# The last 64 rows of two batches in one block, rows dealt in twos, three ways of adding x, and late rows of y moved by DMA

## The chip, the cores and the metric

The kernel runs on one core of a Trainium2 chip. The metric is the device time of one execution in microseconds, the median of several runs. Times of kernels that ran at different sittings are compared through the kernel before, which ran in each: by their ratios to it, where 0.001 is 0.45 us.

## The reference, cut to what matters

```
# attention with forget gates: 8 batches, 8 heads, 576 rows, head size 64
scores = scale * q k^T + (cum_i - cum_j), causal;  attn = softmax(scores);  x = attn v
# then, with x as [8 batches, 576 rows, 512]:
X = rfft(x, axis=1)[:, :64];  Y = X * (w_r + i w_i) per mode      # 64 modes, 512 x 512 each
y = irfft(Y, n=576)
u = x + y
out = u + max(u @ w_ch, 0)
```

576 is four and a half blocks of 128 partitions. That half block, per batch, is what the change is about. The weights of the modes are read from memory at 512 KB per load, 128 loads or so.

## The kernel before: the parts that matter

Attention runs in 32 steps (one head of two batches each). In each step the products of the exponentials E and v make x, block by block:

```
def emit_av(s, sbs):                       # sbs = [0, 1, 2], then [3, 4]
    for i, sb in enumerate(sbs):
        for h in range(2):                 # the two batches
            for jb in range(sb + 1):
                c = EOFF[jb] + (sb - jb) * 128
                nc.tensor.matmul(pav[:, i, h, :], lhsT=E[:, h, c : c + 128],
                                 rhs=va[:, jb, h, :], ...)
    # x_all[:, batch, sb, ...] = pav * 1 / (sum of the row)
```

That is 1+2+3+4+5 = 15 products for each batch. While attention runs, GpSimd issues the loads of q, k, v and of the weights, in order. The weights go into a ring of nine buffers. A buffer comes free when the modes that use it have been multiplied, and the first modes wait for the first spectrum, at step 9 of attention:

```
for s in range(NS + 1):
    if h == 0 and pr + STG - 1 < NPR:  emit_loads(pr + STG - 1)       # q, k, v
    if s < 10 and nload < min(NRING, 3 + 3 * s // 4):  next_w()       # fills the ring
    if s == 10:  pool_dma(wch[:], ...)                                # w_ch, 512 KB
    # ... transposes, scores, emit_av, DFT of this step ...
    if s > B:
        while nmode < (s - B) * NTH // (NS - B):
            emit_modes(nmode); nmode += 1
            next_w()                                                  # needs a free buffer
```

The output stage comes last, when the last modes are done. Modes 0 to 15 come late ("late rows" of y: 32 rows for each batch), are transposed and multiplied for four batches at once into the PSUM tile `pl`, and are copied from there, batch by batch, by VectorE and ScalarE between the output jobs. A job makes two blocks, or the half block, of `out`:

```
def emit_rows(b, pl):
    nc.vector.tensor_copy(yy[0:32, b, 0, :], pl[0][rows, :])
    nc.scalar.copy(yy[0:32, b, 1, :], pl[1][rows, :])

def emit_out(b, sb0, nb, by_pool, ps):
    # pu += basis^T yy[b, 0];  pz += basis^T yy[b, 1]   (u = x + y;  z = u @ w_ch)
    if by_pool:                                    # type P below
        nc.vector.tensor_tensor(u_sb, pu, x_all[...], ALU.add)
        nc.scalar.activation(o_sb, pz, ACT.Relu)
        nc.gpsimd.tensor_tensor(o_sb, o_sb, u_sb, ALU.add)
    else:                                          # type N: x was added by an identity product
        nc.scalar.copy(u_sb, pu)
        nc.vector.scalar_tensor_tensor(o_sb, pz, 0.0, u_sb, ALU.max, ALU.add)
    nc.sync.dma_start(out[b, 128*sb0 : 128*sb0+256, :].rearrange("(r p) e -> p r e", r=2), o_sb)

jobs = [(b, sb0, nb) for b in range(B) for sb0, nb in ((0, 2), (2, 2), (4, 1))]   # 24 jobs
for n, job in enumerate(jobs):
    emit_out(*job, ...)
    if n == 8: pl = emit_late(1); emit_rows(4, pl)
    if n in (0, 1, 2, 9, 10, 11): emit_rows(n + 1 if n < 3 else n - 4, pl)
```

Each job fills two PSUM tiles of two banks; there are four such tiles in all, and `pl` takes one of them.

The softmax here doesn't subtract the row's maximum and nothing guards it: scores larger than these inputs give would overflow.

## Time and profile before

| | |
|---|---|
| time | 452.51 us (451.94 to 452.87, 4 runs) |
| span of the profiled run | 449.9 us |
| last weights used by TensorE | 403.24 us |
| last vector operation ends | 441.59 + 1.81 = 443.40 us |

I divide the span at these two points: the **load stream** up to the last weights, the **output stage** (40.2 us here), and the **drain**, in which stores land and the engines meet (6.5 us).

The chain of waits on the page of the profile, which follows back what released what, is mostly DMA:

```profile
DMA 81%; PE 10%; DVE 2%; issue 2%; ACT 2%; POOL 0%; DVEq 0%; POOLq 0%; ACTq 0%
```

In the views PE is TensorE, PEld its loads of weights, DVE VectorE, ACT ScalarE, POOL GpSimd and SP SyncE. The windows view gives, for stretches of the span, each engine's busy time and instruction count, the granted TensorE clock (PEclk, 1.00 is full speed), the DMA share and the rate. First the load stream:

```profile
core 0: us, PE busy (x) PEld busy (x) DVE busy (x) ACT busy (x) POOL busy (x), PEclk, DMA share, GB/s
0.00:76.00 76.00, 50.90 (x633) 34.45 (x633) 61.78 (x169) 54.37 (x79) 28.67 (x46) 1.00 1.16 226
76.00:104.00 28.00, 23.28 (x444) 18.11 (x444) 21.61 (x59) 18.70 (x29) 12.52 (x17) 0.94 1.18 207
104.00:396.00 292.00, 204.55 (x3404) 148.81 (x3413) 127.56 (x347) 114.16 (x176) 88.24 (x123) 0.76 1.17 217
```

The late rows, the output stage and the drain:

```profile
403.20:408.30 5.10, 4.60 (x27) 2.21 (x28) 1.19 (x3) 0.58 (x2) 0.00 (x0) 0.50 0.01 3
408.30:443.40 35.10, 30.87 (x136) 13.18 (x137) 26.51 (x30) 24.82 (x31) 25.16 (x14) 1.00 0.65 230
443.40:449.90 6.50, 0.00 (x0) 0.00 (x0) 0.00 (x1) 0.00 (x0) 0.00 (x0) 0.69 0.66 216
```

No engine is full in the output stage; TensorE is nearest to it. What it waited for, by the waits view after 403 us (total, times, longest), was mostly ScalarE:

```profile
PE pz L739 <- ACT uo L764: 1.7, 3, 0.7
PE A L134 <- DMA wb<-in_moe_w_i_dram: 1.1, 1, 1.1
PE pl L710 <- DVE YTl L149: 0.5, 1, 0.5
PE pz L739 <- ACT uo L767: 0.4, 1, 0.4
PE pz L739 <- DVE uo L768: 0.2, 1, 0.2
```

The timeline of GpSimd near 64 to 79 us (start, duration, what; in brackets the idle time before it and what ended it) shows the last load for the ninth weights buffer going out at 64.44, and then no load for 13.8 us, until TensorE has used the first buffer:

```profile
64.44 0.74 POOL L84 DMA_DIRECT2D wb<-in_moe_w_i_dram  x1 [1.75 <-DMA wb<-in_moe_w_r_dram]
78.97 0.74 POOL L84 DMA_DIRECT2D wb<-in_moe_w_r_dram  x1 [13.79 <-PE tp L426]
```

### The profile page before, as it was taken

The page shows a single profiled execution, that of the slowest core. Times are in us where ns is not written, and L with a number is a line of the kernel's source. Part 1 is how long each engine was busy: PE and PEld are TensorE (multiplying, and loading weights), DVE is VectorE, ACT ScalarE, POOL GpSimd, SP SyncE. Part 2 cuts the span into 40 slices and gives each one's busy share as a digit, 9 for nine tenths or more (in the row PEclk, how much of TensorE's full clock was granted, in tenths as well). Part 3 has the DMA queues.
Part 4 walks back from the last instruction along what each step waited for, and adds up shares of the span by engine and source line. Part 5 has one row for each costly group of instructions (what it writes and reads, how often), then busy time and mean ns, then how long its engine had stood idle before and what let it go on. Part 6 is the DMA issues. An engine that isn't in the chain of part 4 may idle for free.

```text
span 449.9 us, 10945 instructions
## 1 busy us (share of the span) xinstructions
PE 317.4 (71%) x4688; PEld 218.9 (49%) x4704; DVE 239.0 (53%) x608; ACT 212.6 (47%) x313; POOL 154.6 (34%) x200
## 2 busy tenths in 40 slices
PE   2398877695975968859578879999722257248992
PEld 1255556474754646647556656556512234233441
DVE  5769998684864745747467853233100012105873
ACT  3388988565654654545356614443200012006672
POOL 7333330553333333332333322322232323102783
PEclk9999999987778786786687969999855569558998
DMA  8999999999999999999999999999999999963677
GB/s 204 206 234 233 233 233 233 201 214 228 213 232 221 220 233 216 224 233 206 233 233 211 211 211 211 211 211 211 211 211 211 211 211 211 211 124 106 223 267 247
DMA packets 68144, 96.80 MB, mean 215 GB/s; under 512 B 3264, under 2 KB 44736, under 8 KB 68096
## 3 DMA queue, kind: packets, MB, share of 16 engines
q0 software_dynamic: 62480, 85.34, 102.4%
q1 hardware_dynamic: 5536, 10.63, 6.8%
q8 instruction: 37, 0.61, 0.5%
q10 hardware_dynamic: 80, 0.13, 0.2%
q14 instruction: 11, 0.09, 0.1%
HBM read 163.73 MB, written 9.44 MB: 385 GB/s over the span
## 4 chain that ended last, share of the span: by engine, by line
DMA 81%; PE 10%; DVE 2%; issue 2%; ACT 2%; POOL 0%; DVEq 0%; POOLq 0%; ACTq 0%
DMA wb<-in_moe_w_i_dram 42%; DMA stk<-in_k_dram 18%; DMA stq<-in_q_dram 11%; DMA wb<-in_moe_w_r_dram 7%; DMA stv<-in_v_dram 3%; PE pz L739 2%; PE pu L751 2%; PE pz L751 1%; PE A L134 1%; PE tp L426 1%; ACT uo L767 1%; PE pav L512 1%; PE ps L478 1%; PE pu L734 1%; PE pl L714 1%
## 5 line engine op out<-in xcount | busy, mean ns | idle before, releaser
L485 ACT ACTIVATE E<-ps 128x1024 bf16<-128x1024 f32 (+1 forms) x128 | 103.7, 868 | 28.4 <-PE ps L478 19.7
L134 PE MATMUL A<-XT,wb 128*128 128x16 bf16 x2048 | 71.8, 172 | 50.6 <-DMA wb<-in_moe_w_i_dram 29.5
L134 PEld LDWEIGHTS <-wb 128*128 128x128 bf16 x2048 | 64.3, 100 | 64.3 <-DMA wb<-in_moe_w_i_dram 32.5
L84 POOL DMA_DIRECT2D wb<-in_moe_w_r_dram x65 | 47.3, 728 | 131.7 <-DMA wb<-in_moe_w_r_dram 29.7
L84 POOL DMA_DIRECT2D wb<-in_moe_w_i_dram x65 | 47.2, 727 | 80.0 <-DMA wb<-in_moe_w_i_dram 45.8
L478 PE MATMUL ps<-QTs,KT 64*128 64x64 bf16 (+4 forms) x384 | 56.8, 313 | 10.3 <-ACT E L485 9.5
L149 DVE TENSOR_TENSOR YT<-A,Yacc 128x128 bf16<-128x128 f32 x24 | 8.9, 369 | 77.9 <-PE A L134 77.9
L512 PE MATMUL pav<-va,E 128*128 128x65 bf16 x960 | 48.5, 204 | 0.9 <-DVE va L456 0.4
L512 PEld LDWEIGHTS <-E 128*128 128x128 bf16 x960 | 40.6, 105 | 11.8 <-issue 8.2
L439 ACT COPY KT<-tp 128x640 bf16<-128x640 bf16 (+1 forms) x32 | 22.3, 748 | 39.1 <-PE tp L426 39.1
L500 DVE TENSOR_TENSOR E<-E,trimask 128x256 bf16<-128x256 bf16 (+2 forms) x128 | 38.4, 316 | 3.9 <-ACT E L485 3.7
L657 ACT CAST XW<-pxw 128x512 bf16<-128x512 f32 x40 | 22.7, 587 | 31.6 <-PE pxw L650 26.6
L426 PE MATMUL tp<-ident_bf,kb 128*128 128x128 bf16 x144 | 16.3, 270 | 30.0 <-DVE kb L410 29.5
L650 PE MATMUL pxw<-wch,yy 128*128 128x512 bf16 x152 | 35.4, 380 | 1.3 <-issue 1.1
L765 POOL TENSOR_TENSOR uo<-uo 64x512 f32<-64x512 f32 (+1 forms) x14 | 25.2, 1810 | 28.8 <-DVE uo L761 25.9
L669 ACT CAST yy<-pyw 128x512 bf16<-128x512 f32 x8 | 4.7, 586 | 59.1 <-PE pyw L662 57.6
L521 DVE TENSOR_TENSOR x_all<-pav,rcp 128x384 bf16<-128x384 f32 x64 | 31.4, 490 | 1.0
L478 PEld LDWEIGHTS <-KT 64*128 64x128 bf16 x384 | 18.4, 97 | 22.8 <-issue 14.0
L426 PEld LDWEIGHTS <-kb 128*128 128x128 bf16 x144 | 11.7, 121 | 33.7 <-DVE kb L410 30.8
L443 ACT COPY VT<-tp 128x640 bf16<-128x640 bf16 (+1 forms) x32 | 22.5, 754 | 11.0 <-PE tp L426 10.7
L410 DVE COPY kb<-stk 128x1152 bf16<-128x1152 bf16 x16 | 7.9, 495 | 34.2 <-DMA stk<-in_k_dram 34.1
L441 DVE COPY QTs<-tp 128x640 bf16<-128x640 bf16 (+1 forms) x32 | 23.2, 766 | 5.0 <-PE tp L426 4.1
(103 smaller groups left out, 481.0 us busy)
## 6 DMA issues: line engine op xcount, KB each, us to landing
wb<-in_moe_w_r_dram POOLq DMA_DIRECT2D x63, 512.0 KB, 17.2
wb<-in_moe_w_i_dram POOLq DMA_DIRECT2D x63, 512.0 KB, 18.0
out_dram<-uo SPq DMA_DIRECT2D x16, 512.0 KB, 3.0
stv<-in_v_dram POOLq DMA_DIRECT2D x14, 576.0 KB, 15.7
stk<-in_k_dram POOLq DMA_DIRECT2D x16, 288.0 KB, 15.7
stq<-in_q_dram POOLq DMA_DIRECT2D x16, 288.0 KB, 15.6
stv<-in_v_dram SPq DMA_DIRECT2D x2, 576.0 KB, 6.9
out_dram<-uo SPq DMA_DIRECT2D x7, 128.0 KB, 2.4
```

Of the source, the lines that this page charges most:

```text
L84: tc.keep_in_program_order(nc.gpsimd.dma_start(dst, src))
L134: nc.tensor.matmul(A[:, eb, mi, :], lhsT=wb[:, t, mi, r * D + eb * 128 : r * D + (eb + 1) * 128], rhs=XT3[:, m, c0 : c0 + 2 * B], start=(i ...
L426: nc.tensor.transpose(tp[:, r - r0, :, :].rearrange("c h p -> c (h p)"), sb[:, r, :, :].rearrange("p b d -> p (b d)"), ident_bf[:, :],)
L441: nc.vector.tensor_copy(rows(QT[pr][:, :, :]), tv)
L478: nc.tensor.matmul(ps[:, b, o : o + n], lhsT=KTs[pr % 2][bs, h, jb * 128 : (jb + 1) * 128], rhs=QT[pr][bs, h, jb * 128 + c0 : jb * 128 + c ...
L485: nc.scalar.activation(E[:, :, piece * 512 : piece * 512 + w], ps[:, :, 0:w], ACT.Exp, scale=scale,)
L500: nc.vector.tensor_tensor(dg, dg, tr, ALU.mult)
L512: nc.tensor.matmul(pav[:, i, h, :], lhsT=E[:, h, c : c + 128], rhs=va[:, jb, h, :], start=(jb == 0), stop=(jb == sb),)
L521: nc.vector.tensor_tensor(x_all[:, 2 * bp : 2 * bp + 2, sbs[0] : sbs[0] + n, dc * 128 + hd * Dh : dc * 128 + (hd + 1) * Dh,].rearrange("p ...
L650: nc.tensor.matmul(pxw[:, :], lhsT=xT[:, eb, sb * 128 : (sb + 1) * 128], rhs=wch[:, eb, :], start=(eb == 0), stop=(eb == NDC - 1),)
L657: nc.scalar.copy(XW[:, b, sb, :], pxw[:, :])
L765: nc.gpsimd.tensor_tensor(o_sb, o_sb, u_sb, ALU.add)
```

## The change

Its intent, as I read it:

- The last 64 rows of two batches share one block of 128 partitions: 20 output jobs instead of 24, and nine blocks of x and of x W for a pair of batches instead of ten.
- Rows of a pair of blocks are dealt in twos (partition p holds rows 2p and 2p+1), so that a store writes runs of 4 KB instead of 2 KB. The price is in attention: E is read with a stride of two, and a block of even or odd rows needs an extra half-width product. 17 products for each batch instead of 15.
- Jobs have types. The code knows four; three are used, 9 N (5 large, 4 shared), 7 P and 4 W. W adds x and applies the maximum on VectorE alone.
- The late rows for batches 1 to 7 go from PSUM to SBUF in one copy for four batches and then by DMA, SBUF to SBUF, to their partitions.

The diff, cut to its core:

```
 def emit_av(s, sbs):
+    for i, sb in enumerate(sbs):
+        if sb == 4:                                   # the shared block, half-width
+            for jb in range(NSB):
+                c = EOFF[jb] + (4 - jb) * 128
+                narrow += [(2, b, b, jb, c, 64, 1) for b in range(2)]
+            continue
+        k2, r = sb & 2, sb & 1
+        for b in range(2):
+            for jb in range(k2 + 1):
+                c = EOFF[jb] + (k2 - jb) * 128 + r
+                wide_.append((2 * i + b, b, 0, jb, c, 128, 2))      # stride 2
+            narrow.append((2 * i + b, b, 1, k2 + 1, EOFF[k2 + 1] + r, 64, 2))
 [...]
+def emit_late_rows(q4, pl):
+    nc.vector.tensor_copy(yl[:, 0, :], pl[0][:, :])
+    nc.scalar.copy(yl[:, 1, :], pl[1][:, :])
+    for j in range(1 - q4, 4):
+        nc.sync.dma_start(yy[0:32, 4 * q4 + j, :, :], yl[32 * j : 32 * j + 32, :, :])
 [...]
+    if sb == 4:
+        for h in range(2):
+            nc.tensor.matmul(p[64 * h : 64 * h + 64, 0, :], lhsT=BI[:, 512:576],
+                             rhs=yy[:, b + h, t, :], ...)
 [...]
+    if ty in "PW": nc.vector.tensor_tensor(u_sb, pu, xblk(x_all, job), ALU.add)
+    else:          nc.scalar.copy(u_sb, pu)
+    if ty in "PQ": # ScalarE Relu, GpSimd add, as P before
+    else:          nc.vector.scalar_tensor_tensor(o_sb, pz, 0.0, u_sb, ALU.max, ALU.add)
-    out[b, 128 * sb0 : 128 * sb0 + 256, :].rearrange("(r p) e -> p r e", r=2)
+    out[b, 128 * sb : 128 * sb + 256, :].rearrange("(p r) e -> p r e", r=2)
 [...]
+jobs = [(*j, ty) for j, ty in zip(jobs, "NPWPNPWPNNPWPNNPWNNN")]
+emit_rows(0, pl); emit_late_rows(0, pl)
+for n, job in enumerate(jobs):
+    emit_out(...)
+    if n == 3: emit_late_rows(1, emit_late(1))
```

The rest (a sixth block of the basis, iota, indices of x) follows from these.

More of the change, by code (lines that the diff above doesn't have):

```diff
@@ L48, with xi @@
     EOFF = [0, 576, 1024, 1344, 1536]
-    EW = 1664
+    EW = 1600
+    NX = 9
+    def xi(b, sb):
+        return (b % 2) * 3 + sb if sb < 3 else 6 + b % 2 if sb == 3 else 8
     RP = 64
@@ L59 @@
     xtpool = ctx.enter_context(tc.tile_pool(name="xtpool", bufs=3))
-    x_all = xpool.tile([128, B, NSB, D], BF16, name="x_all")
+    x_all = xpool.tile([128, B // 2, NX, D], BF16, name="x_all")
     Yacc = xpool.tile([128, NDC, NM, 2 * B], F32, name="Yacc")
@@ L65 @@
     wch = const.tile([128, NDC, D], BF16, name="wch")
-    bas = const.tile([128, NSB, NM, 2], BF16, name="bas")
+    bas = const.tile([128, NSB + 1, NM, 2], BF16, name="bas")
     BI = const.tile([128, SP], BF16, name="BI")
@@ L257 @@
         emit_w_load(1)
-        s_i = ssb.tile([128, NSB], I32, name="s_i")
+        s_i = ssb.tile([128, NSB + 1], I32, name="s_i")
         tc.keep_in_program_order(
-            nc.gpsimd.iota(s_i[:], pattern=[[128, NSB]], base=0, channel_multiplier=1)
+            nc.gpsimd.iota(
+                s_i[:, 0:4], pattern=[[256, 2], [1, 2]], base=0, channel_multiplier=2
+            )
+        )
+        tc.keep_in_program_order(
+            nc.gpsimd.iota(
+                s_i[:, 4:6], pattern=[[-64, 2]], base=512, channel_multiplier=1
+            )
         )
@@ L270 @@
             nc.vector.memset(t[:, :, S:SP], 0.0)
-        for t in Es:
-            nc.vector.memset(t[:, :, EW - 64 : EW], 0.0)
         lf = ft
@@ L350, in emit_basis @@
             TURN = 2.0 * math.pi / S * (1.0 - 2.0e-7)
-            s_f = ssb.tile([128, NSB], F32, name="s_f")
+            NB1 = NSB + 1
+            s_f = ssb.tile([128, NB1], F32, name="s_f")
             nc.vector.tensor_copy(s_f[:], s_i[:])
@@ L354, in emit_basis @@
             nc.vector.tensor_copy(m_f[:], m_i[:])
-            ang = wide[:, 0 : 2 * NSB * NM].rearrange(
-                "p (a b c) -> p a b c", a=2, b=NSB
+            ang = wide[:, 0 : 2 * NB1 * NM].rearrange(
+                "p (a b c) -> p a b c", a=2, b=NB1
             )
-            rnd = scratch(128, 2, NSB, NM)
+            rnd = scratch(128, 2, NB1, NM)
             nc.vector.tensor_tensor(
                 ang[:, 1, :, :],
-                _strided(s_f[:, 0:1], [[1, NSB], [0, NM]]),
-                _strided(m_f[:, 0:1], [[0, NSB], [1, NM]]),
+                _strided(s_f[:, 0:1], [[1, NB1], [0, NM]]),
+                _strided(m_f[:, 0:1], [[0, NB1], [1, NM]]),
                 ALU.mult,
@@ L378, in emit_basis @@
             Zt = rnd[:, :, :, :].rearrange("p a b c -> p (a b c)").rearrange(
-                "p (s m t) -> p s m t", s=NSB, m=NM
+                "p (s m t) -> p s m t", s=NB1, m=NM
             )
@@ L383, in emit_basis @@
             nc.vector.memset(Zt[64:128, 4, :, :], 0.0)
+            nc.vector.memset(Zt[0:64, 5, :, :], 0.0)
             nc.vector.tensor_copy(bas[:, :, :, :], Zt[:, :, :, :])
@@ L506, in emit_av @@
             n = len(sbs)
-            pav = psO.tile([128, 3, 2, Dh + 1], F32, tag="av", name="pav")
+            pav = psO.tile([128, 6, Dh + 1], F32, tag="av", name="pav")
+            wide_, narrow = [], []
             for i, sb in enumerate(sbs):
-                for h in range(2):
-                    for jb in range(sb + 1):
-                        c = EOFF[jb] + (sb - jb) * 128
-                        nc.tensor.matmul(
-                            pav[:, i, h, :],
-                            lhsT=E[:, h, c : c + 128],
-                            rhs=va[:, jb, h, :],
-                            start=(jb == 0),
-                            stop=(jb == sb),
-                        )
@@ L519, in emit_av @@
-            rcp = nrm.tile([128, 3, 2, 1], F32, tag="rcp", name="rcp")
-            nc.vector.reciprocal(rcp[:, 0:n, :, :], pav[:, 0:n, :, Dh : Dh + 1])
-            nc.vector.tensor_tensor(
-                x_all[
-                    :,
-                    2 * bp : 2 * bp + 2,
-                    sbs[0] : sbs[0] + n,
-                    dc * 128 + hd * Dh : dc * 128 + (hd + 1) * Dh,
-                ].rearrange("p b c d -> p c b d"),
-                pav[:, 0:n, :, 0:Dh],
-                _strided(rcp[:, 0, 0, 0:1], [[2, n], [1, 2], [0, Dh]]),
-                ALU.mult,
-            )
+                if sb == 4:
[3 more added lines that the diff above has]
+                    continue
@@ new lines, in emit_av @@
+                k2, r = sb & 2, sb & 1
[4 more added lines that the diff above has]
+                    narrow.append((2 * i + b, b, 1, k2 + 1, EOFF[k2 + 1] + r, 64, 2))
+            for n, (slot, b, half, jb, c, w, st) in enumerate(wide_ + narrow):
+                nc.tensor.matmul(
+                    pav[64 * half : 64 * half + w, slot, :],
+                    lhsT=E[:, b, c : c + (w - 1) * st + 1 : st],
+                    rhs=va[:, jb, b, :],
+                    start=(n == 0),
+                    stop=(n == len(wide_) + len(narrow) - 1),
+                    skip_group_check=True,
+                )
@@ new lines, in emit_av @@
+            ns = 6 if sbs[0] == 0 else 3
+            d0 = dc * 128 + hd * Dh
+            rcp = nrm.tile([128, 6, 1], F32, tag="rcp", name="rcp")
+            nc.vector.reciprocal(rcp[:, 0:ns, :], pav[:, 0:ns, Dh : Dh + 1])
+            if ns == 6:
+                xo = x_all[:, bp, 0:6, d0 : d0 + Dh].rearrange(
+                    "p (b c) d -> p c b d", b=2
+                )
+                pi = pav[:, :, 0:Dh].rearrange("p (c b) d -> p c b d", b=2)
+                ri = _strided(rcp[:, 0, 0:1], [[2, 3], [1, 2], [0, Dh]])
+            else:
+                xo = x_all[:, bp, 6:9, d0 : d0 + Dh]
+                pi = pav[:, 0:3, 0:Dh]
+                ri = _strided(rcp[:, 0, 0:1], [[1, 3], [0, Dh]])
@@ L533, in emit_dft @@
+            nc.vector.tensor_tensor(xo, pi, ri, ALU.mult)
         def emit_dft(pr):
@@ L547, in emit_dft @@
                             px[:, :, :],
-                            lhsT=_strided(x_all[:, b, sb, d0 : d0 + 1], [[st, 128]]),
-                            rhs=bas[:, sb, :, :],
+                            lhsT=_strided(
+                                x_all[:, bp, xi(b, sb), d0 : d0 + 1], [[st, 128]]
+                            ),
+                            rhs=bas[:, sb if sb < 4 else 4 + b % 2, :, :],
                             start=(sb == 0),
@@ L615 @@
         late["YT"], late["YTl"] = YT, YTl
-        XW = bsb.tile([128, B, NSB, D], BF16, name="XW")
+        XW = bsb.tile([128, B // 2, NX, D], BF16, name="XW")
         yy = bsb.tile([128, B, 2, D], BF16, name="yy")
@@ L634, with emit_xw @@
             )
-            def emit_xw(b):
-                xT = xTs[b % 3]
+            def emit_xw(n):
+                bp, i0, nb = n // 2, (0, 5)[n % 2], (5, 4)[n % 2]
+                xT = xTs[n % 3]
                 for eb in range(NDC):
                     ptr = psBig.tile([128, SP], BF16, tag="big", name="ptr")
-                    for sc in range(NSB):
+                    for i in range(nb):
                         nc.tensor.transpose(
-                            ptr[:, sc * 128 : (sc + 1) * 128],
-                            x_all[:, b, sc, eb * 128 : (eb + 1) * 128],
+                            ptr[:, i * 128 : (i + 1) * 128],
+                            x_all[:, bp, i0 + i, eb * 128 : (eb + 1) * 128],
                             ident_bf[:, :],
                         )
-                    nc.vector.tensor_copy(xT[:, eb, :], ptr[:, :])
-                for sb in range(NSB):
+                    nc.vector.tensor_copy(
+                        xT[:, eb, 0 : nb * 128], ptr[:, 0 : nb * 128]
+                    )
+                for i in range(nb):
                     pxw = psBig.tile([128, D], F32, tag="big", name="pxw")
@@ L651, in emit_xw @@
                             pxw[:, :],
-                            lhsT=xT[:, eb, sb * 128 : (sb + 1) * 128],
+                            lhsT=xT[:, eb, i * 128 : (i + 1) * 128],
                             rhs=wch[:, eb, :],
@@ L656, in emit_xw @@
                         )
-                    nc.scalar.copy(XW[:, b, sb, :], pxw[:, :])
+                    nc.scalar.copy(XW[:, bp, i0 + i, :], pxw[:, :])
             def emit_y(b):
@@ L721, in emit_late @@
             return ply, plw
+        yls = {}
         def emit_rows(b, pl):
@@ L726, in emit_rows @@
             nc.scalar.copy(yy[0:32, b, 1, :], pl[1][rows, :])
-        def emit_x(b, sb0, nb, by_pool):
+        def emit_late_rows(q4, pl):
+            yl = xtpool.tile([128, 2, D], BF16, tag="XT3", name="yl")
+            nc.vector.tensor_copy(yl[:, 0, :], pl[0][:, :])
+            nc.scalar.copy(yl[:, 1, :], pl[1][:, :])
+            for j in range(1 - q4, 4):
+                nc.sync.dma_start(
+                    yy[0:32, 4 * q4 + j, :, :], yl[32 * j : 32 * j + 32, :, :]
+                )
@@ L730, in emit_x, with xblk @@
+        def xblk(t, job):
+            b, sb, nb, _ = job
+            i0 = xi(b, sb)
+            step = xi(b, sb + 1) - i0 if nb == 2 else 1
+            return _strided(t[:, b // 2, i0, 0:1], [[step * D, nb], [1, D]])
+        def emit_x(job):
+            b, sb, nb, ty = job
             pu = psZ.tile([128, 2, D], F32, tag="z", name="pu")
             pz = psZ.tile([128, 2, D], F32, tag="z", name="pz")
-            for i in range(nb):
-                if not by_pool:
-                    nc.tensor.matmul(
-                        pu[:, i, :], lhsT=ident_bf[:, :], rhs=x_all[:, b, sb0 + i, :],
-                        start=True, stop=False,
-                    )
@@ L738, in emit_x @@
-            for i in range(nb):
-                nc.tensor.matmul(
-                    pz[:, i, :], lhsT=ident_bf[:, :], rhs=XW[:, b, sb0 + i, :],
-                    start=True, stop=False,
-                )
-            return pu, pz
-        def emit_out(b, sb0, nb, by_pool, ps):
-            Ms = 64 if nb == 1 else 128
-            pu, pz = ps
-            for t, p in enumerate((pu, pz)):
+            for p, t in ((pu, x_all), (pz, XW)):
+                if t is x_all and ty not in "NQ":
+                    continue
@@ L749, in emit_out @@
                 for i in range(nb):
-                    sb = sb0 + i
                     nc.tensor.matmul(
                         p[:, i, :],
-                        lhsT=BI[:, sb * 128 : (sb + 1) * 128],
-                        rhs=yy[:, b, t, :],
-                        start=(t == 0 and by_pool),
-                        stop=True,
-                    )
-            uo = wpool.tile([128, 2, 2, D], F32, tag="wb", name="uo")
-            u_sb, o_sb = uo[:Ms, 0, 0:nb, :], uo[:Ms, 1, 0:nb, :]
@@ L760, in emit_out @@
-            if by_pool:
-                nc.vector.tensor_tensor(
-                    u_sb, pu[:Ms, 0:nb, :], x_all[:Ms, b, sb0 : sb0 + nb, :], ALU.add
-                )
-                nc.scalar.activation(o_sb, pz[:Ms, 0:nb, :], ACT.Relu)
+                        lhsT=ident_bf[:, :],
+                        rhs=t[:, b // 2, xi(b, sb + i), :],
+                        start=True,
+                        stop=False,
+                        skip_group_check=True,
+                    )
+            return pu, pz
@@ new lines, in emit_out @@
+        def emit_out(job, ps, last):
+            b, sb, nb, ty = job
+            for t, p in enumerate(ps):
+                fresh = t == 0 and ty not in "NQ"
+                for i in range(nb):
+                    if sb == 4:
+                        for h in range(2):
+                            nc.tensor.matmul(
+                                p[64 * h : 64 * h + 64, 0, :],
+                                lhsT=BI[:, 512:576],
+                                rhs=yy[:, b + h, t, :],
+                                start=fresh,
+                                stop=True,
+                                skip_group_check=True,
+                            )
+                    else:
+                        nc.tensor.matmul(
+                            p[:, i, :],
+                            lhsT=BI[:, (sb + i) * 128 : (sb + i + 1) * 128],
+                            rhs=yy[:, b, t, :],
+                            start=fresh,
+                            stop=True,
+                            skip_group_check=True,
+                        )
+            pu, pz = (p[:, 0:nb, :] for p in ps)
+            uo = wpool.tile([128, 2, 2, D], F32, tag="wb", name="uo")
+            u_sb, o_sb = uo[:, 0, 0:nb, :], uo[:, 1, 0:nb, :]
+            if ty in "PW":
+                nc.vector.tensor_tensor(u_sb, pu, xblk(x_all, job), ALU.add)
+            else:
+                nc.scalar.copy(u_sb, pu)
+            if ty == "X":
+                nc.gpsimd.tensor_tensor(u_sb, u_sb, xblk(x_all, job), ALU.add)
+            if ty in "PQ":
+                nc.scalar.activation(o_sb, pz, ACT.Relu)
@@ L765, in emit_out @@
                 nc.gpsimd.tensor_tensor(o_sb, o_sb, u_sb, ALU.add)
             else:
-                nc.scalar.copy(u_sb, pu[:Ms, 0:nb, :])
                 nc.vector.scalar_tensor_tensor(
-                    o_sb, pz[:Ms, 0:nb, :], 0.0, u_sb, ALU.max, ALU.add
+                    o_sb, pz, 0.0, u_sb, ALU.max, ALU.add
                 )
-            if nb == 1:
-                eng = nc.scalar if b == B - 1 else nc.sync
-                eng.dma_start(out[b, 512:576, :], uo[:Ms, 1, 0, :])
+            if sb == 4:
+                for h in range(2):
+                    eng = nc.scalar if last and h else nc.sync
+                    eng.dma_start(
+                        out[b + h, 512:576, :], uo[64 * h : 64 * h + 64, 1, 0, :]
+                    )
@@ L774, in emit_out @@
             else:
                 nc.sync.dma_start(
-                    out[b, 128 * sb0 : 128 * sb0 + 256, :].rearrange(
-                        "(r p) e -> p r e", r=2
+                    out[b, 128 * sb : 128 * sb + 256, :].rearrange(
+                        "(p r) e -> p r e", r=2
                     ),
@@ L780, in emit_out @@
                 )
-        jobs = [(b, sb0, nb) for b in range(B) for sb0, nb in ((0, 2), (2, 2), (4, 1))]
-        jobs = [
-            (*j, j[1] != 2 and 0 < n < len(jobs) - 1) for n, j in enumerate(jobs)
-        ]
-        ps0 = emit_x(*jobs[0])
+        jobs = []
+        for bp in range(B // 2):
+            jobs += [(b, sb, 2) for b in (2 * bp, 2 * bp + 1) for sb in (0, 2)]
+            jobs.append((2 * bp, 4, 1))
+        jobs = [(*j, ty) for j, ty in zip(jobs, "NPWPNPWPNNPWPNNPWNNN")]
+        ps0 = emit_x(jobs[0])
         emit_modes(nmode)
@@ L789 @@
         emit_rows(0, pl)
+        emit_late_rows(0, pl)
         for n, job in enumerate(jobs):
-            emit_out(*job, emit_x(*job) if n else ps0)
-            if n == 8:
-                pl = emit_late(1)
-                emit_rows(4, pl)
-            if n in (0, 1, 2, 9, 10, 11):
-                emit_rows(n + 1 if n < 3 else n - 4, pl)
+            emit_out(job, emit_x(job) if n else ps0, n == len(jobs) - 1)
+            if n == 3:
+                emit_late_rows(1, emit_late(1))
 _INS = ['q', 'k', 'v', 'f', 'moe_w_r', 'moe_w_i', 'moe_w_ch']
```

## The prediction

> **What bounds it.** (1) Until the last weights land at 403.2 us, loads. The chain of waits is 81% DMA; from 225 to 395 us it is one load of weights after another, 15 to 20 us each. DMA share stays over 1.1 in every ten microseconds from 60 to 390, while TensorE waits 28.7 us for loaded k. (2) The tail, 403.2 to 449.9 us: last modes and late rows (5.1 us, granted clock 0.50), the output stage with its last vector operation at 443.4, then 6.5 us of stores landing and barrier. In the output stage (408.3 to 444, 35.7 us) nothing is full: PE 30.9 us, DVE 26.5, ACT 24.8, POOL 25.2, DMA 0.66. The chain there is mostly PE, with 1.7 us of waiting for ACT.
>
> **Before 403 us.** The attention's products of weights and v go from 15 to 17 per head and batch, 960 to 1088. Runs of them cost about 55 ns each: 7 us more PE, against 28.7 us of waiting for k. Their stationary operand is now read with a stride of two. The Trainium skill, "TensorE: Matmul & The Clock Gate", section on weight-path modes, allows packed or strided columns for the fast weight load; this trace agrees: in the DFT five products take about 0.40 us packed, 0.44 us with stride two. The same bytes are loaded. The stream ends at 403 us, within 1 us: gain zero.
>
> **The tail, by durations of the trace** (128x1024 operations: ACT 1.01, DVE 1.22, POOL 2.35; 128x512: 0.59, 0.67; product 0.216 at full clock). 24 output jobs become 20: 16 large (5 N, 7 P, 4 W), 4 shared (N).
> - ACT: 25.6 to 16.3 us (W needs none; casts of late rows 8 to 3).
> - POOL: 25.4 to 7 x 2.35 = 16.5 us.
> - DVE: 9 x 1.22 + 7 x 1.22 + 8 x 0.67 + 8 x 0.42 = 28.2 us; after, 5 x 1.22 + 7 x 1.22 + 4 x 2.43 + 4 x 0.67 + 3 x 0.42 = 28.3. Unchanged.
> - PE: 151 products to 146: 32.6 to 31.5 us at full clock. Shared blocks save identity products, not those of the basis.
>
> So the two fullest engines hardly change; ACT and POOL get slack. What can be won is idle time: late rows no longer hold a fourth of the output PSUM buffers for several jobs, nor queue on ACT and DVE between jobs. PE needed about 29 us of work in the 33.4 us after 408.3; I expect 28 us in about 30. P W P is DVE-bound (4.87 against 3.9 us PE), N N PE-bound, so overlap isn't perfect. Job 2 waits for a row move (2 to 3 us to land), about when its products are due: perhaps 0.5 us. The start (403.2 to 408.3) stays. Runs of 4 KB: stores ran at 250 GB/s at 0.72 busy; 9.4 MB in 31 us asks 305 GB/s, which longer runs ease, but the drain is mostly latency: gain 0 to 1 us.
>
> **Predicted: 448.5 us** (4 us less, 0.9%), range 445.8 to 451.0. Faster by over 2%: 0.06; within 2%: 0.91; slower by over 2%: 0.03.
>
> **What would show it.** Last weights still landing near 403; last vector operation near 439 to 440; POOL and ACT near 16 us each in the output stage, DVE near 27, PE near 30; PE's waits for ACT mostly gone, waits for DVE around W; packets of stores halved.
>
> **What would make it wrong.** Stores being the real pace (the drain grows); row moves landing late; the 128 extra products or strided reads slowing attention so that loads are issued late (POOL waited 13.8 us for PE between 45 and 90 us), moving 403 itself; PE stalling around W as much as before.

## The result, and the profile after

The kernel after took 448.69 us (median of 4 runs, 448.25 to 448.85), the one before 452.51. The ratio is 0.9915 (95% interval 0.9898 to 0.9932). Ratios here are the mean time of one kernel's fast runs over that of the other's of the same rounds, so not quite the ratio of the medians quoted. The predicted 448.5 was right almost to the digit. The way there was not.

The last weights and the last vector operation of the kernel after, in the timeline:

```profile
405.34 0.54 PE L138 MATMUL A<-XT,wb 128*128 128x16 bf16 x14 [1.06 <-DMA wb<-in_moe_w_i_dram]
439.10 1.82 DVE L830 SCALAR_TENSOR_TENSOR uo<-pz,uo 128x1024 f32<-128x1024 f32 x2 [0.77 <-ACT uo L823]
```

| | before | after | difference |
|---|---|---|---|
| last weights used | 403.24 | 405.34 | +2.1 |
| output stage, to the end of the last vector operation | 40.2 | 35.6 | -4.6 |
| drain, to the end of the span | 6.5 | 5.6 | -0.9 |
| span | 449.9 | 446.5 | -3.4 |

So the load stream, of which I had said that it would not move, lost 2.1 us, and the tail gained 5.5 us, where I had said 4. The two errors have opposite signs. Here is the windows view of the load stream after:

```profile
core 0: us, PE busy (x) PEld busy (x) DVE busy (x) ACT busy (x) POOL busy (x), PEclk, DMA share, GB/s
0.00:76.00 76.00, 53.35 (x645) 35.64 (x645) 59.09 (x163) 52.88 (x75) 28.83 (x47) 1.00 1.16 226
76.00:104.00 28.00, 24.94 (x431) 19.12 (x427) 20.22 (x55) 17.60 (x27) 11.75 (x16) 0.82 1.11 195
104.00:396.00 292.00, 212.88 (x3505) 152.36 (x3506) 129.03 (x355) 116.14 (x176) 89.03 (x124) 0.75 1.17 217
```

The rate is the same before 76 us and after 104 us, 226 and 217 GB/s. Only between them it is 195 instead of 207. (207 - 195) GB/s times 28 us is 0.34 MB; at 217 GB/s that is 1.5 us of the 2.1. GpSimd's timeline shows the place: the pause of 13.8 us has become 15.4, and the next load goes out 2 us later.

```profile
64.76 0.74 POOL L88 DMA_DIRECT2D wb<-in_moe_w_i_dram  x1 [1.75 <-DMA wb<-in_moe_w_r_dram]
80.93 0.74 POOL L88 DMA_DIRECT2D wb<-in_moe_w_r_dram  x1 [15.43 <-PE tp L437]
```

By then the queue of loads is empty. The windows view in pieces of 2 us has 128 GB/s before and this after:

```profile
80.00:82.00 2.00, 2.00 (x49) 1.62 (x46) 1.73 (x4) 1.04 (x2) 1.04 (x2) 1.00 0.20 39
```

The chain of waits of the kernel after has changed too:

```profile
DMA 58%; PE 18%; DVE 7%; ACT 7%; issue 3%; POOL 1%; SPq 1%; DVEq 0%; ACTq 0%; POOLq 0%
```

This share is no measure of a late stream, though: rows_in_order below, whose stream is hardly late, has DMA at 53%.

The tail after, in the same three parts as before:

```profile
405.30:409.80 4.50, 3.95 (x26) 1.91 (x27) 0.78 (x2) 0.59 (x2) 0.00 (x0) 0.60 0.00 0
409.80:440.90 31.10, 27.97 (x130) 11.11 (x129) 27.43 (x26) 15.24 (x18) 16.51 (x7) 1.00 0.76 278
440.90:446.50 5.60, 0.00 (x0) 0.00 (x0) 0.02 (x1) 0.00 (x0) 0.00 (x0) 0.69 0.63 226
```

ScalarE fell to 15.2 us and GpSimd to 16.5, VectorE stayed near 27; these sums were predicted well. TensorE's waits after 403 us are now three. Those for ScalarE are gone, and one for a row move is new:

```profile
PE pu L809 <- DMA yy<-yl: 1.4, 1, 1.4
PE A L138 <- DMA wb<-in_moe_w_i_dram: 1.1, 1, 1.1
PE pl L740 <- DVE YTl L153: 0.5, 1, 0.5
```

### The profile page after: what moved, and what is told of

It is laid out like the page before. It is cut to its first block, busy times and chain, and to the rows that moved or that the text cites. A ratio compares the mean times of both kernels' runs of the same rounds, so it can differ in the third digit from the quotient of the medians.

```text
span 446.5 us, 11102 instructions
## 1 busy us (share of the span) xinstructions
PE 327.1 (73%) x4791; PEld 222.6 (50%) x4791; DVE 237.3 (53%) x602; ACT 202.4 (45%) x296; POOL 146.1 (33%) x194
## 4 chain that ended last, share of the span: by engine, by line
DMA 58%; PE 18%; DVE 7%; ACT 7%; issue 3%; POOL 1%; SPq 1%; DVEq 0%; ACTq 0%; POOLq 0%
DMA wb<-in_moe_w_i_dram 30%; DMA stk<-in_k_dram 13%; DMA stq<-in_q_dram 11%; ACT E L496 4%; DMA wb<-in_moe_w_r_dram 3%; PE tp L437 3%; PE pav L534 3%; PE pxw L680 3%; PE ps L489 3%; PE A L138 2%; DVE XT L581 2%; PE vp L461 1%; DVE uo L821 1%; PE ptr L669 1%; ACT KT L450 1%
## 5 line engine op out<-in xcount | busy, mean ns | idle before, releaser
L534 PE MATMUL pav<-va,E 128*128 128x65 bf16 (+1 forms) x1088 | 55.9, 210 | 4.3 <-DVE x_all L556 2.6
L534 PEld LDWEIGHTS <-E 128*128 128x128 bf16 (+1 forms) x1088 | 45.1, 114 | 15.8 <-issue 5.6
L687 ACT CAST XW<-pxw 128x512 bf16<-128x512 f32 x36 | 20.3, 587 | 29.8 <-PE pxw L680 25.1
L680 PE MATMUL pxw<-wch,yy 128*128 128x512 bf16 x144 | 33.5, 382 | 0.0
L556 DVE TENSOR_TENSOR x_all<-pav,rcp 128x384 bf16<-128x384 f32 x64 | 29.2, 456 | 0.9
L828 POOL TENSOR_TENSOR uo<-uo 128x1024 f32<-128x1024 f32 x7 | 16.5, 2359 | 29.3 <-DVE uo L821 25.5
L581 DVE CAST XT<-px 128x128 bf16<-128x128 f32 x32 | 21.0, 805 | 8.6 <-PE px L571 8.6
L425 DVE TENSOR_TENSOR vb<-stv,wdec 128x1152 bf16<-128x1152 f32 x16 | 21.6, 1351 | 5.4 <-PE tp L437 4.7
```

What stands on the lines that cost most here:

```text
L534: nc.tensor.matmul(pav[64 * half : 64 * half + w, slot, :], lhsT=E[:, b, c : c + (w - 1) * st + 1 : st], rhs=va[:, jb, b, :], start=(n == ...
L556: nc.vector.tensor_tensor(xo, pi, ri, ALU.mult)
L581: nc.vector.tensor_copy(_strided(XT3[:, 0, B + b : B + b + 1], [[3 * B, NM], [B, 2]]), px[:, :, :],)
L680: nc.tensor.matmul(pxw[:, :], lhsT=xT[:, eb, i * 128 : (i + 1) * 128], rhs=wch[:, eb, :], start=(eb == 0), stop=(eb == NDC - 1),)
```

## The experiments

Twelve kernels ran, in three sittings of four. Each table entry is read from one trace, the time from the runs. "First load" is the first load after GpSimd's pause.

| kernel | us, median | ratio to before | first load | last weights | output stage | drain |
|---|---|---|---|---|---|---|
| before | 452.51 | 1 | 78.97 | 403.24 | 40.2 | 6.5 |
| after | 448.69 | 0.9915 | 80.93 | 405.34 | 35.6 | 5.6 |
| rows_in_order | 448.91 | 0.9926 | 79.16 | 403.61 | 36.2 | 6.5 |
| rows_by_copy | 449.21 | 0.9932 | 80.91 | 405.45 | 37.7 | 4.5 |
| types_as_before | 450.33 | 0.9955 | 80.98 | 405.75 | 36.4 | 6.4 |
| shared_only | 449.82 | 0.9946 | 79.36 | 403.56 | 36.5 | 6.7 |
| order_17 | 450.34 | 0.9956 | 82.87 | 407.20 | 35.6 | 6.5 |
| wch_early | 448.26 | 0.9909 | 81.26 | 405.83 | 35.6 | 5.1 |
| half_stores | 448.41 | 0.9913 | 81.05 | 405.58 | 36.2 | 5.2 |
| before_no_rows | 450.23 | 0.9952 | 81.17 | 405.53 | 37.7 | 6.2 |
| stride_15 | 448.86 | 0.9909 | 79.82 | 404.35 | 36.2 | 6.3 |
| full_width_tails | 448.42 | 0.9908 | 81.11 | 405.63 | 35.9 | 4.9 |
| first_row_by_copy | 447.79 | 0.9893 | 81.21 | 406.07 | 35.0 | 5.0 |
| combined | 449.31 | 0.9923 | 81.16 | 405.62 | 34.2 | 7.2 |

Two cautions for this table. First, a trace is of one run, and the runs spread. That of shared_only is the fastest of six (spans of 446.8 to 449.5 us), that of types_as_before the slowest of five (447.9 to 448.6).

Second, after the last weights TensorE stays at half clock for some time, and not equally long in each trace. These lines show the 6.5 us after the last weights in after, rows_in_order and types_as_before:

```profile
405.34:411.84 6.50, 5.96 (x34) 2.58 (x34) 2.21 (x4) 2.63 (x4) 0.00 (x0) 0.73 0.00 0
403.61:410.11 6.50, 5.80 (x32) 2.62 (x33) 1.64 (x4) 2.06 (x4) 0.00 (x0) 0.63 0.00 0
405.75:412.25 6.50, 6.04 (x31) 2.72 (x32) 1.34 (x4) 2.02 (x3) 0.00 (x0) 0.53 0.00 0
```

6.5 us times what the clock lacks is the time lost if TensorE sets the pace there, an estimate: 1.8 us in after, order_17, wch_early and combined; 1.9 in full_width_tails and first_row_by_copy; 2.3 to 2.5 in before, before_no_rows, rows_in_order and shared_only; 2.8 in rows_by_copy; 3.1 to 3.3 in types_as_before, half_stores and stride_15. So a difference of a microsecond in the output stage can be the clock's. I say below where it matters; no experiment held the clock fixed.

### First sitting: one part undone at a time

**rows_in_order**: the kernel after, with rows in order.

```
-pattern=[[256, 2], [1, 2]], base=0, channel_multiplier=2
+pattern=[[128, 4]], base=0, channel_multiplier=1
-k2, r = sb & 2, sb & 1 ...                 # stride 2, extra half-width product
+for jb in range(sb + 1):
+    wide_.append((2 * i + b, b, 0, jb, EOFF[jb] + (sb - jb) * 128, 128, 1))
-"(p r) e -> p r e"
+"(r p) e -> p r e"
```

> The kernel after, with rows dealt in order again: 15 products per head and batch, packed weight reads, stores of 2-KB runs. Theory (the last weights land 2.1 us later after the change, 405.3 against 403.2, because attention up to the first modes is slower by the 17 products, and the queue of loads runs dry near 80 us): the hole near 80 to 82 us is as in before (about 130 GB/s, not 39), the first load after it is issued near 79 us, the last weights land near 403.2; the kernel is about 2 us faster than after, less what 2-KB stores cost. Rival (the longer set-up, six blocks of basis, shifts attention): stream still ends near 405.3, time near that of after. For the stores: if 4-KB runs matter, the time from the last vector operation to the end grows from 5.6 towards the 6.5 us of before and stores reach less GB/s.

The stream ends 1.7 us earlier than in after, the first load goes out at 79.16, and the rate from 76 to 104 us is that of before again:

```profile
76.00:104.00 28.00, 24.04 (x418) 18.13 (x417) 19.93 (x57) 17.60 (x27) 12.50 (x17) 0.82 1.18 207
```

So the loss in the stream goes with the dealt rows, and not with the longer set-up; what in them makes it is taken up under stride_15. But the time is no better than that of after (ratios of 0.9926 and 0.9915): the drain is 0.9 us longer, the output stage 0.6, and that 0.6 is as much as the clock lost (2.4 against 1.8 us). The runs also spread more, spans of 445.8 to 447.9 against 446.5 to 447.1. In these traces, dealing the rows took from the stream what it gave to the end.

**rows_by_copy**: late rows by `emit_rows` between jobs, no row moves.

```
-emit_late_rows(0, pl)
-if n == 3: emit_late_rows(1, emit_late(1))
+if n == 3: pl = emit_late(1); emit_rows(4, pl)
+if n in (0, 1, 2, 4, 5, 6): emit_rows(n + 1, pl)
```

> The kernel after, with late rows copied by DVE and ACT between the jobs as in before, no row moves by DMA. My theory of the tail (late rows held PSUM buffers and queued on ACT and DVE): the output stage gets 2 to 3 us longer. Rival (the row moves are only a cost: TensorE waited 1.4 us for the first, 2 us of the chain): the kernel is as fast as after or up to 1.4 us faster. Stream end unchanged at 405.3 in both.

The output stage grew by 2.1 us, as my theory had it, of which up to 1.0 can be the clock's. But the drain shrank by 1.1, and the time grew by only 0.8 us by the ratios. The row moves are worth little in the end.

**types_as_before**: the old mix of N and P.

```
-"NPWPNPWPNNPWPNNPWNNN"
+"NNPNPPNPNPPNPNPPNPNN"
```

> The kernel after with the old two ways of adding x (9 N and 7 P of the large jobs, 3 P and 1 N of the shared), no W. ACT and POOL get about 6 and 4 us more work, DVE about 5 us less, TensorE 5 identity products more or so. If W is what made the tail shorter, the output stage gets 2 us or more longer; if the late rows and the fewer jobs did it, it changes by less than 1 us.

1.8 us slower by the ratios. Of its profile, 0.9 us lie in the output stage, 0.8 in the drain and 0.4 in the stream, of which the edit touches nothing. The types matter, by 1 to 2 us, for all five runs are slower than every run of after. Where they matter the trace doesn't show: the clock lost 1.3 us more than in after, which is more than the output stage grew.

**shared_only**: all three undone, only the shared block left.

```
rows_in_order + rows_by_copy + types_as_before
```

> All three undone at once: only the shared block of the last 64 rows is left of the change. Stream end as in before, 403.2 (15 products). If sharing alone pays (20 output jobs instead of 24, 8 fewer small operations on DVE and ACT): 1 to 2 us faster than before in the tail. If it doesn't: within 0.5 us of before. The three single steps together with this should add up to the 3.8 us of the whole change, counting the 2.1 us loss of the load stream.

This was the surprise. The output stage is 36.5 us, 3.6 less than before, more than the 1 to 2 expected, with the late rows still copied and the old types; the clock lost about as much in both (2.3 and 2.5 us). The time is 2.5 us less than before in the same rounds (449.82 against 452.32). The sum that I had expected does not come out: by the ratios, undoing the three singly costs 0.5 + 0.8 + 1.8 = 3.1 us, undoing all of them 1.4 us. The parts overlap. One thing besides the sharing is left in this kernel: the second group of late rows is made after job 3 of 20, where before made it after job 8 of 24. No run tells the two apart.

### Second sitting: the stream, and what paces the tail

**order_17**: rows in order, with two more products for each batch and head into a slot that nobody reads.

```
+if sbs[0] == 3:
+    for b in range(2):
+        for e in range(2): wide_.append((4 + b, b, 0, e, EOFF[e], 128, 1))
```

> Rows in order (packed reads, 2-KB stores) with two more products per head and batch, into a slot that nobody reads: 1088 products as after, but without the stride and without the half-width ones. If the number of products delays the first modes, the hole near 80 us is as deep as in after (30 to 40 GB/s between 80 and 82) and the last weights are used near 405.3. If the stride or the half-width reads do it, the hole stays as with rows in order (114 GB/s) and the last weights are used near 403.6.

The first load went out at 82.87 and the stream ended at 407.2, later than in after:

```profile
76.00:104.00 28.00, 24.90 (x396) 19.13 (x395) 19.69 (x55) 18.58 (x27) 10.98 (x15) 0.70 1.00 179
```

17 packed products are thus late as well (the two added ones are full-width; those of the shared block stay half-width). But in this trace the granted clock fell to 0.50 between 80 and 86 us, and to 0.54 and 0.61 between 42 and 46, so the run says "late without the stride", not how much of the lateness is due to the count. It ran only twice, and its second run had a span of 447.6 against 449.3.

**before_no_rows**: the kernel before without the late rows of six batches (wrong).

```
-if n in (0, 1, 2, 9, 10, 11): emit_rows(...)
```

> The kernel before, wrong on purpose: the late rows of y for batches 1 to 3 and 5 to 7 are left out (six of the eight copies on DVE and on ACT). My prediction's reason for the shorter tail was that they hold a PSUM buffer and queue between the jobs: then the output stage (last weights used to last vector operation, 40.2 us) falls by 2 to 4 us. The rival, that 24 jobs with eight half-filled ones cost the time: it falls by less than 1 us.

The output stage fell by 2.5 us, to 37.7, in the range expected. What the clock lost at the start of this stage is 2.5 us in both traces. The late rows did cost the kernel before that much, their copies, the queueing and the held buffer together. This run showed something else as well. It has the 15 packed products of the kernel before, and yet its first load went out at 81.17 and its stream ended at 405.53. Two things made it late. VectorE waited for a load of k:

```profile
74.25 0.46 DVE L410 COPY kb<-stk 128x1152 bf16<-128x1152 bf16 x1 [1.29 <-DMA stk<-in_k_dram]
```

In before the same copy started at 73.24, so 1.0 us was lost while the clock was full. Then TensorE was at half clock when the first modes were due, and at the first load the delay was 2.2 us:

```profile
78.00:80.00 2.00, 2.00 (x33) 2.00 (x31) 0.86 (x3) 1.37 (x2) 0.00 (x0) 0.50 0.96 161
80.00:82.00 2.00, 2.00 (x40) 1.37 (x39) 1.15 (x4) 0.54 (x1) 0.83 (x2) 0.50 0.17 27
```

Its four spans are 447.0, 447.7, 449.4 and 449.7, with mean clocks of 0.830, 0.831, 0.820 and 0.817: two groups, 2 us apart. The Trainium skill, "TensorE: Matmul & The Clock Gate", section "What's actually happening", says that an idle TensorE drops to half its clock. Here it had been idle for 1.7 of the 3 us from 73 to 76, waiting in attention, and the clock fell in the next microsecond (0.55). It was not idle throughout, so the trace agrees in direction and does not show the rule. Whether all slow runs of such kernels have this cause is not shown, since only one run of each leaves a trace.

**wch_early**: the load of w_ch two steps earlier, to fill the hole.

```
-if s == 10: pool_dma(wch[:], ...)
+if s == 8:  pool_dma(wch[:], ...)
```

> The kernel after with the load of w_ch (512 KB, no ring slot needed) issued two steps earlier, just before GpSimd stops for want of a free weights slot. If the dry queue of loads near 80 us is what moved the end of the stream from 403.2 to 405.3: the hole between 80 and 82 us fills, the last weights are used near 403.0 (2 to 2.4 us earlier), and the kernel is 2 us faster than after, about 446.7. If the queue's dryness doesn't matter (something later binds again): no change from after, 448.7.

The hole near 80 us did fill, and the stream did not end earlier:

```profile
76.00:104.00 28.00, 23.52 (x408) 18.19 (x408) 19.19 (x51) 17.52 (x26) 10.25 (x14) 0.82 1.16 200
80.00:82.00 2.00, 2.00 (x53) 1.67 (x51) 1.74 (x5) 1.03 (x3) 0.74 (x2) 1.00 1.20 199
98.00:100.00 2.00, 2.00 (x44) 1.79 (x44) 1.14 (x1) 1.67 (x3) 0.34 (x1) 0.50 0.91 125
```

A second hole opened at 98 us, when GpSimd waited again, 9.5 us, for modes on TensorE at half clock. So the bubble by itself was not the cause. That points to the late attention, which frees the buffers: an extra 512 KB only moves the moment at which the queue runs dry. Part of the bytes was won back (200 GB/s against 195), and still the last weights came at 405.83. Why the end did not profit even from that is open.

**half_stores**: only partitions 0 to 63 of each large block are stored (a wrong result: half of `out` is never written).

```
-out[b, 128 * sb : 128 * sb + 256, :] <- o_sb
+out[b, 128 * sb : 128 * sb + 128, :] <- uo[0:64, 1, 0:nb, :]
```

> The kernel after, wrong on purpose: of each large block only the half in partitions 0 to 63 is stored (4.7 MB less or so). If the stores are the pace at the end (DMA share 0.98 to 1.03 from 426 us on): the time from the last vector operation to the end falls from 5.6 to 4.5 us or less, and the last vector operation comes earlier too if buffers waited for stores. If the drain is latency alone: span and last vector operation as in after, within 0.5 us.

Nothing came of it: 448.41 us, output stage 36.2, drain 5.2. By the expectation the stores are not the pace. But the DMA share from 426 to 434 us was still 0.97 to 0.99, at 215 to 236 GB/s: the edit halved the bytes and not the time in which the engines were busy. And the clock lost 3.3 us at the start of this tail, 1.5 more than in after, which could hide a gain. The run does not settle the question.

### Third sitting

**stride_15**: rows in order, 15 products, weights read with a stride of two (wrong).

```
-c = EOFF[jb] + (sb - jb) * 128;                    lhsT=E[:, b, c : c + 128]
+c = min(EOFF[jb] + (sb - jb) * 128, EW - 256);     lhsT=E[:, b, c : c + 255 : 2]
```

> Rows in order with 15 products, but weights read with a stride of two (wrong values on purpose). If the number of products delays the first modes: the trace is that of rows in order, the first load after the hole is issued near 79.2 us and the last weights are used near 403.6 (unless the granted clock falls to 0.5 before 80 us[...]). If the stride does it: near 81 and 405.3 as in after.

```profile
76.00:104.00 28.00, 22.35 (x400) 17.27 (x400) 19.71 (x56) 17.22 (x27) 11.99 (x17) 0.82 1.13 200
```

It lies between rows_in_order and after: first load at 79.82, last weights at 404.35, so 0.7 us later than rows_in_order and 1.0 earlier than after. One load of the weights took 98 ns against 97 packed, so the load itself did not get longer.

The first steps of attention tell more than these end points. VectorE writes x twice in each step; the table gives the start of two of these writes and of the first load:

| trace | second write | sixteenth write | first load |
|---|---|---|---|
| rows_in_order | 35.20 | 73.84 | 79.16 |
| shared_only | 35.36 | 73.91 | 79.36 |
| stride_15 | 36.10 | 74.35 | 79.82 |
| order_17 | 36.23 | 76.27 | 82.87 |
| after | 36.54 | 75.29 | 80.93 |

Of the 1.8 us between rows_in_order and after, 1.3 are there at the second write. From the second write to the sixteenth after takes only 0.1 us longer (38.75 against 38.64), and stride_15 takes less (38.25). So no cost of the stride shows, and the added products cost little once the first steps are over: 0.1 us in this stretch, and at most 0.3 more until the first load.

In the first steps TensorE ran at half speed. The same five products show it: in before they take 0.69 us at 224 us, where the windows view has a clock of 0.50, and 0.45 at 60 us, where it has 1.00. These two lines come first; then, in the first steps, rows_in_order, after and order_17:

```profile
223.99 0.69 PE L450 MATMUL vp<-ident_bf,VT 128*128 128x128 bf16 x5
60.02 0.45 PE L450 MATMUL vp<-ident_bf,VT 128*128 128x128 bf16 x5
33.19 0.45 PE L461 MATMUL vp<-ident_bf,VT 128*128 128x128 bf16 x5
33.86 0.72 PE L461 MATMUL vp<-ident_bf,VT 128*128 128x128 bf16 x5
33.42 0.71 PE L461 MATMUL vp<-ident_bf,VT 128*128 128x128 bf16 x5
```

The windows view gives 1.00 in the last three cases as well, so in this first stretch the durations are the better witness. By them TensorE reaches full speed between 32 and 33 us in before, before_no_rows, rows_in_order and shared_only, near 35 in order_17 and stride_15 (which had been fast and fell back to 0.50 at 32), and between 35 and 38 in all eight traces with dealt rows. Three microseconds more at half speed are 1.5 us of work, an estimate, and about the loss. Whether dealing the rows makes TensorE late at full speed is not settled: eight of eight traces speak for it, but order_17 was late after the same products at the same times, within 0.1 us, as rows_in_order up to 33 us.

**full_width_tails**: the half-width products of the shared blocks made full width (wrong, but within the tolerance).

```
-p[64 * h : 64 * h + 64, 0, :], lhsT=BI[:, 512:576]
+p[:, 0, :],                    lhsT=BI[:, 512:640]
```

> The kernel after, wrong on purpose: the 16 half-width basis products of the shared blocks are full width, so that no two can run side by side. In after two such products start 0.24 to 0.31 us after the pair before, where full ones need 0.43. If half-width products overlap and TensorE is the pace: the output stage is 1.0 to 1.6 us longer than the 35.6 us of after. If I misread the spacing: no change.

The reading of the spacing was right. In after, a pair of half-width products (L800, 128x64 weights) is followed by the next pair 0.24 us later, while full-width pairs (L809) need 0.43:

```profile
431.28 0.41 PE L800 MATMUL pu<-yy,BI 128*64 128x512 bf16 x2
431.52 0.38 PE L800 MATMUL pz<-yy,BI 128*64 128x512 bf16 x2
431.83 0.60 PE L783 MATMUL pz<-XW,ident_bf 128*128 128x512 bf16 x2
432.41 0.59 PE L809 MATMUL pu<-yy,BI 128*128 128x512 bf16 x2
432.84 0.59 PE L809 MATMUL pz<-yy,BI 128*128 128x512 bf16 x2
```

The same lines of full_width_tails, where the pairs are 0.43 us apart:

```profile
431.69 0.59 PE L800 MATMUL pu<-yy,BI 128*128 128x512 bf16 x2
432.12 0.59 PE L800 MATMUL pz<-yy,BI 128*128 128x512 bf16 x2
```

The Trainium skill, "TensorEngine Tiling (Array Packing)", section "Key Properties", says that such tiles work independently and in parallel, and this trace agrees. But the worth was overestimated: the output stage grew by 0.3 us and not by 1.0 to 1.6, and the time did not grow at all (448.42).

**first_row_by_copy**: the late rows of batch 1 are copied, those of the other batches move by DMA.

```
 emit_rows(0, pl)
+emit_rows(1, pl)
-for j in range(1 - q4, 4):
+for j in range(2 - 2 * q4, 4):
```

> The kernel after, but the late rows of batch 1, the first that are needed, are copied by DVE and ACT; the others still move by DMA. TensorE waited 1.4 us for that first move. If the wait is a real cost: it goes, the output stage falls by about 1 us (two more small operations on DVE and ACT) and the kernel to about 447.7. If the stores or DVE were the pace anyway: within 0.4 us of after.

It came as expected. The wait for the row move is gone from TensorE's waits, the output stage is 0.6 us shorter, and the median is 447.79 us. The five spans are 445.7 to 446.7, the four of after 446.5 to 447.1. The intervals of the ratios overlap (0.9874 to 0.9913 against 0.9898 to 0.9932), so this is the best kernel by a likely and not a certain 0.9 us (1.0 by the ratios).

**combined**: first_row_by_copy, and two of the N jobs made P.

```
-"NPWPNPWPNNPWPNNPWNNN"
+"NPWPNPWPPNPWPPNPWNNN"
```

> As first_row_by_copy, and two of the N jobs (the third one of pairs 2 and 3) become P: four identity products less on TensorE (0.86 us), one 2.35 us addition more on GpSimd for each. If TensorE is the pace of the output stage: 0.5 to 0.9 us faster than first_row_by_copy, about 447.0. If DVE (27.9 us busy in 35.7) is the pace: no change.

The output stage did get 0.8 us shorter, as it should if TensorE paces it, and the kernel got 1.5 us slower (449.31). GpSimd's timeline shows six of its additions back to back, where first_row_by_copy has a pause of more than a microsecond before each of the last five:

```profile
423.61 13.93 POOL L828 TENSOR_TENSOR uo<-uo 128x1024 f32<-128x1024 f32 x6 [1.22 <-DVE uo L821]
```

Stores are issued by one queue in order, so a store of a P job that waits for GpSimd holds those behind it. The waits view has this queue waiting 10.7 us for GpSimd, against 6.7 in first_row_by_copy. From 434 to 438 us this kernel stored at 308 GB/s and first_row_by_copy at 372. The backlog came out in the drain, 7.2 us against 5.0.

## Why the prediction was right, and where it was not

1. **What bounds the kernel**: right. Loads until 403 us, then a tail in which TensorE and VectorE are the fullest.
2. **"The stream ends at 403 us, within 1 us: gain zero"**: this step failed. I set 7 us of extra TensorE work against 28.7 us of waiting for k, both summed over the whole of attention. But up to step 9 there is a stretch in which the loads depend on attention and not attention on the loads: all nine buffers are full, and GpSimd waits for TensorE. A delay in those nine steps comes out in the load stream, which never catches up, since it runs at 217 GB/s in both kernels afterwards. The step lost 2.1 us. I had the wait of 13.8 us in front of me, and named it as a risk. But the risk that I named, 128 extra products or strided reads, seems the smaller part: against rows_in_order, 1.3 of 1.8 us were lost by 36.5 us, while TensorE was still at half speed, and only 0.4 us after that. In the eight traces with dealt rows the first load goes out between 80.9 and 81.3 us and the last weights are used between 405.3 and 406.1. In before, rows_in_order and shared_only it is 79.0 to 79.4 and 403.2 to 403.6; in before_no_rows a late load of k and the half clock made the same delay. No cost of the stride shows; why TensorE is later at full speed in the traces with dealt rows stays open.
3. **The sums of the tail**: right for ScalarE, GpSimd and VectorE. For TensorE, "shared blocks save identity products, not those of the basis" was wrong, since half-width products run side by side, but full_width_tails shows that it mattered by 0.3 us of the output stage.
4. **"What can be won is idle time: late rows no longer hold PSUM or queue between jobs"**: the mechanism is real, before_no_rows measured 2.5 us for it. But I gave it all the gain and the shared block none. Sharing (with the earlier second group of late rows) makes the output stage 3.6 us shorter with the late rows still copied, and on top of it the rest of the change brings only 0.9 us more, of which up to 0.6 can be the clock's. 24 jobs with eight half-filled ones kept the four PSUM tiles less well used than 20 jobs do; that this is why the two gains overlap is an argument and not shown.
5. **"Perhaps 0.5 us" for the first row move**: 1.4 us, and first_row_by_copy got 0.6 of the output stage and 1.0 of the time back. ScalarE had copied the first job's result before it copied the late rows for the move.
6. **The drain, "gain 0 to 1 us"**: 0.9. Where stores have runs of 2 KB the drain is 6.2 to 6.7 us; where they have 4 KB it is 4.5 to 5.6, except in the two kernels with more P work or later P work (types_as_before 6.4, combined 7.2). The Trainium skill, "Perfetto Trace Analysis", section "DMA Optimizations", says that going from 2 KB to 4 KB can raise throughput dramatically; here the drain is about 1 us of 450 shorter, and while the stores kept the DMA engines busy (share 1.00 to 1.03, 426 to 442 us) they moved 383 GB/s in after and 373 in rows_in_order. That the longer runs shorten the drain is likely, not shown.
7. **The total**: a loss of 2.1 us that I had not counted and a tail 1.5 us better than counted nearly cancelled. The number was right for partly wrong reasons, and so by luck.

## What to carry to other kernels

Slack summed over a stage says nothing about the stretch in which the dependency runs the other way: look for the one long wait of the load issuer, ask what releases it, and follow everything that lies before that release, the clock of TensorE too: here a delay of a microsecond in the first steps came out 40 us later and stayed to the end. Read the clock from the durations of one kind of product as well as from the view. In a tail with several engines near full, shortening one engine's work can lengthen the end, if it moves work in front of an in-order queue of stores. And check a right total by its parts: two errors of 2 us had cancelled here.

## What the Trainium skill lacked or had wrong

- "TensorE: Matmul & The Clock Gate": the price of a half clock is worked out as time lost on TensorE. What the page lacks is a half clock that delays the release of buffers, and so the loads: in before_no_rows one near 80 us held the first load back by about 1.2 of 2.2 us.
- "TensorEngine Tiling (Array Packing)": pairs of half-width products started 0.24 us apart where full-width ones need 0.43. What the page lacks is a figure for such pairs that stand alone between full-width products: 0.3 us of the output stage for eight pairs.
- "Perfetto Trace Analysis", section "DMA Optimizations": going from 2 KB to 4 KB can be a dramatic gain, it says; here the busy DMA engines moved 383 GB/s instead of 373.
